# Decode attention over two caches: moving score products from the matrix engine's path to the vector path, with row sums on ScalarE

## The chip, the cores and the metric

One core of a Trainium2 chip runs the whole program. The metric is the device time of one execution in microseconds (us). Engines are named as in the profile: PE (matmul), PEld (its weight loads), DVE (VectorE), ACT (ScalarE), POOL (GpSimd) and SP (here only the issuer of the loads). "DMA engine" always means one of the 16 that move the data.

## The reference

Two independent attentions, A and B, each decode one token: 32 heads, 8192 cached keys of 128 numbers, bf16. The outputs of both are laid side by side.

```python
q = (x @ wq).reshape(B, 1, 32, 128).transpose(0, 2, 1, 3)   # x: 1 x 1 x 512
scores = einsum("bhqd,bhkd->bhqk", q, k_cache) * 128 ** -0.5 # k_cache: 1 x 32 x 8192 x 128
p = softmax(scores)
o = einsum("bhqk,bhkd->bhqd", p, v_cache)
out = o.transpose(0, 2, 1, 3).reshape(B, 1, 4096) @ wo       # wo: 4096 x 512
# result: concatenate([out_A, out_B], -1), 1 x 1 x 1024
```

Every cached byte is used once: K and V are 2 MB per head each, for 64 heads; with wq and wo that is 285 MB.

## The kernel before

The 64 heads are numbered through. Scores are made in rounds of 8 heads; one softmax serves a round. SP issues all loads in one order: in step g the V of head g - 12, then the K of head g, and once in a round one wo block of 1 MB. Four K slots and four V slots lie in SBUF.

Scores of a head go one of two ways. On **path P**, PE transposes K (64 tiles of 128x128), ACT copies the result out of PSUM, PE multiplies with q. On **path D** K stays as it is: it is multiplied by q, replicated over the partitions, and each group of 128 products is summed. POOL multiplies four of eight chunks, DVE the other four, and DVE sums all eight.

```python
def _default_path(NG, G, LAG):
    pre = "PDPDPPDPDPDP"                     # first 12 heads
    ...                                      # then every fourth head P: 20 P, 44 D in all

def load_v(g):
    if g >= NV:
        W('SP', c_pv, pv_val[g - NV])        # slot is free when PV of head g-4 is done
    ...
def load_k(g):
    if g >= NK:
        for ctr, val in k_free[g - NK]:      # slot is free when head g-4 has been multiplied / transposed
            W('SP', ctr, val)
    ...

def plan_D_step(g, u):                       # u = 0..7, one chunk each
    ...
    # DVE: chunks 4..7 multiplied, one per u     -> ybufe, "dmul"
    # POOL: chunks 0..3 multiplied, one per u    -> ybuf,  "mul"
    # DVE: chunk u summed with tensor_reduce     -> s_sb,  "red"

def plan_sm_tr(r, m1v):                      # softmax of round r, on PE
    W('PE', c_m1, m1v)                       # waits for DVE's maxima of all 8 heads
    ...
    OP('PE', lambda e: e.transpose(misc[:, 0:P], m1pad[:], ident_f[:])...)

def plan_PV(g, first, count):                # p times V of a head: 2 of 16 matmuls per u, on PE
    ...                                      # the last one frees V slot g % 4
```

In the timelines of this case PE runs its instructions in program order (at the tail, below, it stands idle for 6.73 us before the transpose although later PV matmuls need nothing from it).

## Time and profile before

| | before |
|---|---|
| time given, median of 4 runs | 687.79 us (687.55 to 688.66) |
| span of the profiled run, mean granted PE clock | 686.9 us, 0.807 |
| bytes loaded | 285.2 MB |
| share of the span in which the main load queue was busy | 99.0% |

The first fence has lines of the page: busy time, share of the span and instruction count of each engine; then two rows of 40 equal slices of the span (mean busy share of the DMA engines in tenths, and GB/s); then the DMA queues with packets, MB and share.

```profile
PE 447.7 (65%) x4107; PEld 265.4 (39%) x4163; DVE 525.4 (76%) x640; ACT 269.8 (39%) x534; POOL 372.1 (54%) x190
DMA  8999999999999999999999999999999999999995
GB/s 333 424 412 411 427 425 405 432 426 427 426 426 417 427 429 424 428 413 426 426 428 429 413 426 427 428 418 423 427 425 428 408 427 428 427 429 394 426 429 238
q1 hardware_dynamic: 28868, 285.23, 99.0%
q8 instruction: 33, 0.54, 0.3%
q14 instruction: 14, 0.11, 0.0%
```

No compute engine is close to full, and the loads are: the DMA share is 9 tenths or more in 38 of 40 slices. The Trainium skill ("Perfetto Trace Analysis", section Roofline) gives a core's 16 DMA engines about 435 GB/s together; the best slice here has 432, so the trace agrees. Two lines, q8 and q14, carry the instructions of the engines themselves. They are 0.65 MB of 286.

The second view is the groups of instructions (line, engine, operation, output and input with shapes, count; then busy us and mean ns of one; then idle time before them and what ended it).

```profile
L503 POOL TENSOR_TENSOR ybuf<-kn,qbc 128x1024 bf16<-128x1024 bf16 x176 | 367.8, 2121 | 246.2 <-DMA kn<-in_B_k_cache_dram 127.4
L512 DVE TENSOR_REDUCE s_sb<-ybuf 128x8 f32<-128x1024 bf16 x176 | 212.4, 1207 | 19.1 <-POOL ybuf L503 19.1
L524 DVE TENSOR_REDUCE s_sb<-ybufe 128x8 f32<-128x1024 bf16 x176 | 202.0, 1201 | 0.0
```

DVE's sums are the costliest thing it does: 414 of its 525 us. They would be the bottleneck if more heads went on path D. POOL mostly waits for K.

### The profile page before, as it was taken

What the parts mean: (1) busy time and instruction counts of PE and PEld (TensorE: products, weight loads), DVE (VectorE), ACT (ScalarE), POOL (GpSimd) and SP (SyncE); (2) the same over time, 40 slices, a digit from 0 to 9 for tenths busy, and PEclk for the clock granted to TensorE, in tenths of its full rate; (3) what the DMA queues carried; (4) which work ended last, traced back from release to release, by engine and by line L of the source; (5) the groups of instructions that cost most, each with busy time, mean ns of one, the idle gap of its engine ahead of it and who ended that gap; (6) DMA issues with size and microseconds to landing.
All of it is one profiled execution on the core that took longest, in us unless ns stands there. A gap on an engine that the chain in (4) does not pass through costs nothing.

```text
span 686.9 us, 10246 instructions
## 1 busy us (share of the span) xinstructions
PE 447.7 (65%) x4107; PEld 265.4 (39%) x4163; DVE 525.4 (76%) x640; ACT 269.8 (39%) x534; POOL 372.1 (54%) x190
## 2 busy tenths in 40 slices
PE   1577557845776658676566656675577654848985
PEld 1466555422524224252333325243253422415433
DVE  0356779999897897969989696996979789796001
ACT  0548657422625233262431426133262423415410
POOL 2434667567482755836486473845838376590000
PEclk9967857988698878788787887678778787887999
DMA  8999999999999999999999999999999999999995
GB/s 333 424 412 411 427 425 405 432 426 427 426 426 417 427 429 424 428 413 426 426 428 429 413 426 427 428 418 423 427 425 428 408 427 428 427 429 394 426 429 238
DMA packets 28915, 285.88 MB, mean 416 GB/s; under 512 B 3266, under 2 KB 11460, under 8 KB 11460
## 3 DMA queue, kind: packets, MB, share of 16 engines
q1 hardware_dynamic: 28868, 285.23, 99.0%
q8 instruction: 33, 0.54, 0.3%
q14 instruction: 14, 0.11, 0.0%
HBM read 285.21 MB, written 0.00 MB: 415 GB/s over the span
## 4 chain that ended last, share of the span: by engine, by line
DMA 49%; DVE 19%; PE 16%; issue 7%; ACT 5%; POOL 2%; SPq 1%; another core or an unknown queue 0%; ACTq 0%; DVEq 0%
DMA kn<-in_B_k_cache_dram 32%; DMA kn<-in_A_k_cache_dram 11%; DVE s_sb L512 9%; PE acc L716 8%; DVE s_sb L524 5%; DMA vn<-in_B_v_cache_dram 4%; PE ktps L409 4%; DVE ybufe L485 4%; ACT ktsb L418 3%; POOL ybuf L503 2%; PE misc L848 2%; DMA vn<-in_A_wq_dram 2%; DVE m1pad L599 1%; PE sps L442 1%; ACT ptmp L658 1%
## 5 line engine op out<-in xcount | busy, mean ns | idle before, releaser
L503 POOL TENSOR_TENSOR ybuf<-kn,qbc 128x1024 bf16<-128x1024 bf16 x176 | 367.8, 2121 | 246.2 <-DMA kn<-in_B_k_cache_dram 127.4
L716 PE MATMUL acc<-vn,pt 128*128 128x512 bf16 x939 | 274.7, 430 | 9.9 <-DMA vn<-in_B_v_cache_dram 5.1
L512 DVE TENSOR_REDUCE s_sb<-ybuf 128x8 f32<-128x1024 bf16 x176 | 212.4, 1207 | 19.1 <-POOL ybuf L503 19.1
L524 DVE TENSOR_REDUCE s_sb<-ybufe 128x8 f32<-128x1024 bf16 x176 | 202.0, 1201 | 0.0
L418 ACT COPY ktsb<-ktps 128x1024 bf16<-128x1024 bf16 x160 | 158.5, 1015 | 86.0 <-PE ktps L409 81.1
L409 PE MATMUL ktps<-ident,kn 128*128 128x128 bf16 x1280 | 126.9, 260 | 98.4 <-DMA kn<-in_B_k_cache_dram 60.3
L485 DVE TENSOR_TENSOR ybufe<-kn,qps 128x1024 bf16<-128x1024 bf16 x176 | 117.9, 670 | 63.1 <-issue 36.4
L409 PEld LDWEIGHTS ktps<-ident,kn 128*128 128x128 bf16 x1280 | 104.9, 119 | 141.1 <-DMA kn<-in_B_k_cache_dram 64.2
L716 PEld LDWEIGHTS acc<-vn,pt 128*128 128x128 bf16 x992 | 97.7, 109 | 107.2 <-issue 37.2
L796 ACT CAST accsb<-acc 4x512 bf16<-4x512 f32 x62 | 35.7, 576 | 218.6 <-PE acc L716 218.2
L442 PE MATMUL sps<-q_sb,ktsb 128*128 128x8 bf16 (+1 forms) x1280 | 57.1, 169 | 2.5 <-ACT ktsb L418 1.9
L442 PEld LDWEIGHTS sps<-q_sb,ktsb 128*128 128x128 bf16 x1280 | 52.3, 100 | 9.4 <-ACT ktsb L418 6.0
L689 ACT ACTIVATE pt<-ptmp,rinv 128x64 bf16<-128x64 f32 x64 | 16.1, 334 | 65.6 <-DVE rinv L676 65.6
L831 DVE CAST ot_pad<-misc 128x4 bf16<-128x4 f32 (+1 forms) x16 | 2.7, 168 | 39.9 <-PE misc L814 39.9
L848 PE MATMUL misc<-wo_sb,ot_pad 128*128 128x512 bf16 x62 | 22.3, 526 | 12.7 <-DVE ot_pad L831 12.7
L609 PE MATMUL misc<-ident_f,m1pad 128*128 128x128 f32 x8 | 3.5, 438 | 32.6 <-DVE m1pad L599 32.6
L374 PE MATMUL misc<-diag,ones_bf 128*128 128x512 bf16 (+3 forms) x14 | 5.1, 361 | 24.0 <-ACT diag L366 24.0
L334 PE MATMUL acc<-xT,vn 128*128 128x1 bf16 x256 | 7.1, 165 | 19.4 <-DMA vn<-in_A_wq_dram 14.9
L366 ACT ACTIVATE diag<-ident,q 128x128 bf16<-128x128 bf16 x44 | 14.5, 393 | 12.5 <-DVE q L348 12.5
L562 PE MATMUL qps<-ident,qrep 128*128 128x128 bf16 x44 | 4.0, 227 | 21.7 <-ACT qrep L545 21.7
L848 PEld LDWEIGHTS misc<-wo_sb,ot_pad 128*128 128x128 bf16 x64 | 7.5, 125 | 26.5 <-DVE ot_pad L831 15.2
L609 PEld LDWEIGHTS misc<-ident_f,m1pad 128*128 128x128 f32 x8 | 1.4, 172 | 36.3 <-DVE m1pad L599 36.3
(44 smaller groups left out, 123.2 us busy)
## 6 DMA issues: line engine op xcount, KB each, us to landing
kn<-in_A_k_cache_dram SPq DMA_DIRECT2D x32, 2048.0 KB, 22.5
vn<-in_A_v_cache_dram SPq DMA_DIRECT2D x32, 2048.0 KB, 23.4
kn<-in_B_k_cache_dram SPq DMA_DIRECT2D x32, 2048.0 KB, 27.8
vn<-in_B_v_cache_dram SPq DMA_DIRECT2D x32, 2048.0 KB, 23.6
vn<-in_A_wq_dram SPq DMA_DIRECT2D x1, 4096.0 KB, 12.9
vn<-in_B_wq_dram SPq DMA_DIRECT2D x1, 4096.0 KB, 17.4
wo_sb<-in_A_wo_dram SPq DMA_DIRECT2D x4, 1024.0 KB, 25.8
wo_sb<-in_B_wo_dram SPq DMA_DIRECT2D x4, 1024.0 KB, 29.6
```

The lines of the kernel that those rows point to most:

```text
L366: ins = e.activation(diag[:, db, i, :], ident[:], AF.Copy, scale=q32[:, h_:h_ + 1])
L409: last = e.transpose(ktps[:, bank, i * P:(i + 1) * P], kn[:, slot, t, :], ident[:])
L418: OP('ACT', lambda e, bank=bank, ks_slot=ks_slot: e.copy(ktsb[:, ks_slot, :], ktps[:, bank, :]).then_inc(c_e.sem, 1), "evac(%d,%d)" % (g, u))
L442: last = e.matmul(sps[:, sb, col:col + nn], ktsb[:, ks_slot, i * P:(i + 1) * P], q_sb[:, g:g + 1].broadcast_to([P, nn]), start=True, stop= ...
L485: OP('DVE', lambda e, slot=slot, es=es, i=i, qs=qs: e.tensor_tensor(ybufe[:, es], kn[:, slot, i * CH:(i + 1) * CH, :], qps[:, None, qs * P ...
L503: OP('POOL', lambda e, slot=slot, ys=ys, i=i, buf=buf, qi=qi: e.tensor_tensor(ybuf[:, ys], kn[:, slot, i * CH:(i + 1) * CH, :], qbc[:, buf ...
L512: OP('DVE', lambda e, ys=ys, rb=rb, j=j, i=i: e.tensor_reduce(s_sb[:, rb, j, i * CH:(i + 1) * CH], ybuf[:, ys], AX.X, ALU.add).then_inc(c_ ...
L524: OP('DVE', lambda e, es=es, rb=rb, j=j, i=i: e.tensor_reduce(s_sb[:, rb, j, i * CH:(i + 1) * CH], ybufe[:, es], AX.X, ALU.add).then_inc(c ...
L689: OP('ACT', lambda e, r=r, j=j, rb=rb: e.activation(pt[:, rb, j * NT:(j + 1) * NT], ptmp[:, rb, j, :], AF.Copy, scale=rinv[:, r, j:j + 1], ...
L716: last = e.matmul(acc[:, ob, :], pt[:, rb, j * NT - 32 * (j % XG) + c * PVC:j * NT - 32 * (j % XG) + c * PVC + P], vn[:, slot, c * PVC:(c ...
L796: OP('ACT', lambda e, ob=ob, xb=xb, k=k: e.copy(accsb[32 * k:32 * k + PVC, xb, :], acc[32 * k:32 * k + PVC, ob, :]).then_inc(c_ac.sem, 1), ...
L848: last = e.matmul(misc[:, 0:NOUT], ot_pad[:, g - r * G, :], wo_sb[:, r % 2, g - r * G, :], start=(i == 0), stop=(i == n - 1),)
```

## The change

The intent: nearly all heads go on path D (58 instead of 44; only heads 0, 2, 4, 6, 8 and 10 stay on P), which takes transposes off PE and copies off ACT. To make room on DVE, ACT sums two of the eight chunks, tile by tile, with `accum_out` (16 tiles per head, two instructions each). The four DVE multiplies move to the head's start, and the sums of POOL's chunks are planned a step later. The loads are not touched. In the cut below `LAG` is 12, `u` is one eighth of a head's step.

```diff
 def _default_path(NG, G, LAG):
-    pre = "PDPDPPDPDPDP"
     out = []
     for g in range(NG):
-        if g < len(pre):
-            out.append(pre[g])
+        if g < LAG:
+            out.append("P" if g % 2 == 0 else "D")
         else:
-            out.append("P" if ((g - len(pre)) % 4 == 3) else "D")
+            out.append("D")
 ...
+    ARC: int = 2,          # chunks of a head that ACT sums
+    ARC_PRE: int = 0,      # the same for the first NPRE heads
+    NPRE: int = 12,
 ...                        # in plan_D_step:
-            if DSTEP <= u < DSTEP + DVC:
-                i = NPC + (u - DSTEP)      # one DVE multiply per u
+            if u == 0:
+                for e_ in range(DVC):      # all four at u == 0
+                    i = NPC + e_
 ...
-                W('DVE', c_mul, mv)        # sum right after POOL's multiply
+                pend_red.append((g, n, i)) # sum a step later
 ...
+            for e_ in range(ARCg):
+                if u == min(UPH - 1, 1 + 2 * e_):
+                    i = NPC + e_
+                    ...
+                    for tt in range(CH):   # 8 tiles of 128 columns
+                        OP('ACT', lambda e, ...: e.activation(
+                            junk_a[:, ja, :], ybufe[:, es, tt, :], AF.Copy,
+                            accum_out=s_sb[:, rb, j, t:t + 1],
+                        ).then_inc(c_ared.sem, 1), "ared(%d,%d)" % (g, t), 2)
+            for e_ in range(ARCg, DVC):    # the other chunks: DVE tensor_reduce as before
 ...
```

## The prediction

> **What bounds it now.** The DMA. The page's slice row gives a DMA share of 9 tenths or more in 38 of 40 slices, mostly about 427 GB/s, and the main queue is busy 99.0% of the span with 285.2 MB. The Trainium skill ("Perfetto Trace Analysis", Roofline) gives about 435 GB/s for a core's 16 DMA engines; the best slice here reaches 432, so there is no headroom. The chain of waits repeats every 81.7 us: a round of 8 heads, K and V and one wo, at 424 GB/s, 10.2 us per head. In such a round the windows view shows DVE busy 71 us, PE 53 (clock 0.8), POOL 50, ACT 30.5: none is full, except DVE in an early round (79.3 of 81.7).
>
> **The change.** Path P (PE transposes, ACT evacuations) falls from 20 heads to 6, path D (POOL and DVE multiply, then reduce) rises from 44 to 58; from head 12 on all are D, and there ACT sums two of eight chunks instead of DVE. The four DVE multiplies move to the head's start. No byte of DMA changes.
>
> **Costs, from the timeline's pitches.** A 128x1024 reduction issues every 1.13 us, a DVE multiply every 0.59, a POOL multiply takes 2.12 (2.110 to 2.137).
> - DVE, D head: before 8 x 1.13 + 4 x 0.59 = 11.4 us; after 6 x 1.13 + 4 x 0.59 = 9.1. Round: 73 + 2.5 of softmax and output + 1 to 3 of waits = 77 to 79.
> - POOL: 68 per round.
> - ACT: exp pairs (activate 64 columns, accumulator read) issue every 0.336 us. "ScalarE: Activation LUTs" (What ACT_TABLE_LOAD costs) says 0.833 ns per element; my estimate for 128 columns is 0.39. Sixteen tiles: 6.2 us per head, 65 per round with the rest. 8.1 us of evacuations per P head go.
> - PE: 2560 transposes and QK matmuls become 768, off the path.
>
> All stay below 81.7, so the middle stays DMA-bound. DVE will run 2 to 10 us behind K's landing; four K buffers (about 40 us) hide that.
>
> **Ends.** First 12 heads: D takes 11.4 to 14 us per two heads against 9.8 of K; DVE falls 8 to 10 us behind and recovers later. Head 8 (P) now gates K12: its transposes wait behind round 0's maximum, which waits for D7, so K12 is issued near 93 us with the queue almost dry: 0 to 2 us lost, in place of the dip before (DMA share 0.96 at 102 to 119 us). The last head becomes D: the last softmax ends 0 to 4 us later, but V60's load needs the PV of head 56 only by about 9 us later than it came before. The end still follows the last V's landing (682 us).
>
> **Prediction:** 688.0 us, 8 in 10 within 685.5 to 692. Faster by over 2%: 0.01; within 2%: 0.94; slower by over 2%: 0.05.
>
> **What would show it.** DMA share 9 in nearly all slices; rounds of 81 to 82 us; per round DVE busy about 76, ACT 65, POOL 68; ACT sum pairs at 0.3 to 0.4 us; SP still waiting mostly for PV.
>
> **What would make it wrong.** ACT tiles at 0.55 us or more (accumulator read not overlapped) would fill ACT with 90 us a round and bound the kernel; DVE waits of over 6 us a round (multiplies waiting for ACT to free buffers, softmax steps queued behind ACT sums) would make DVE the bound; POOL slowed by the DVE bursts; a larger DMA gap near 95 us.

## The result, and the profile after

| | before | after |
|---|---|---|
| median | 688.28 us of 13 (687.55 to 689.78) | 694.81 us of 8 (693.75 to 695.3) |
| ratio | | 1.0094 (95%: 1.0084 to 1.0104) |
| span of the profiled run, PE clock | 686.9 us, 0.807 | 693.2 us, 0.763 |

All ratios in this document are the mean time of one kernel's runs over that of the kernel before in the same rounds, so not quite the ratio of the medians beside them. Executions over 1.5% slower than the fastest of the same kernel are left out of the means. The change costs 6.5 us, clear of the noise (the interval of the ratio lies above 1), and the prediction's range (685.5 to 692) does not hold it.

The same lines of the page after:

```profile
PE 369.5 (53%) x2356; PEld 180.9 (26%) x2385; DVE 569.3 (82%) x704; ACT 413.5 (60%) x2114; POOL 489.1 (71%) x246
DMA  8999999999999999999999999999999899999995
GB/s 335 424 412 414 425 419 428 428 427 428 426 428 413 428 429 425 428 415 426 427 429 419 421 427 430 425 415 427 429 426 427 317 432 427 429 421 390 360 428 222
q1 hardware_dynamic: 28868, 285.23, 98.3%
q8 instruction: 19, 0.31, 0.2%
q14 instruction: 27, 0.22, 0.1%
```

The same load packets, the same MB, and still no full engine. But one slice near 545 us has 317 GB/s and one from 641 to 659 us has 360. And the two instruction queues have changed places: 14 packets fewer on q8, 13 more on q14.

The groups after:

```profile
L519 POOL TENSOR_TENSOR ybuf<-kn,qbc 128x1024 bf16<-128x1024 bf16 x232 | 484.8, 2122 | 143.2 <-DMA kn<-in_B_k_cache_dram 64.6
L551 ACT ACTIVATE junk_a<-ybufe 128x128 bf16<-128x128 bf16 x832 | 243.7, 294 | 116.3 <-DVE ybufe L501 116.3
L530 DVE TENSOR_REDUCE s_sb<-ybuf 128x8 f32<-128x1024 bf16 x232 | 271.8, 1207 | 29.3 <-POOL ybuf L519 29.2
L551 ACT ACTIVATION_READ_ACCUMULATOR junk_a<-ybufe 128x1 f32 x832 | 155.2, 186 | 0.0
L566 DVE TENSOR_REDUCE s_sb<-ybufe 128x8 f32<-128x1024 bf16 x128 | 148.4, 1202 | 0.0
```

The compute came out as intended: DVE's sums take 420 us where they took 414, though 14 more heads use them; POOL's multiply is unchanged at 2122 ns; with its sums ACT is busy for 60% of the span.

**When did the bytes arrive?** The trace has a record of every DMA packet, so one can ask at which time X MB had landed:

```
MB landed            40     45    100    225    230    260    265    270    275   285.2
before, us        99.69 112.40 241.90 536.77 549.06 619.43 632.04 644.26 655.94 681.22
after - before    +0.28  -0.77  -0.84  -1.17  +2.71  +2.44  +3.37  +5.15  +5.62  +5.93
```

After the change the kernel is *ahead* for 540 us. It then loses 3.9 us within 5 MB (545 to 552 us), and about 3 us more between 630 and 650. Everything else is neutral. So two short places need explaining, not the middle.

**The first place: SP's queue.** The timeline of SP, before: start, duration, the issue. Its last line is the next load after the wait.

```profile
520.30 0.43 SPq L258 DMA_DIRECT2D wo_sb<-in_B_wo_dram  x1
528.38 16.44 SPq L258 DMA_DIRECT2D vn<-in_B_v_cache_dram  x1
544.92 0.38 SPq L258 DMA_DIRECT2D kn<-in_B_k_cache_dram  x1
```

And after:

```profile
524.74 0.43 SPq L263 DMA_DIRECT2D wo_sb<-in_B_wo_dram  x1
533.51 15.27 SPq L263 DMA_DIRECT2D vn<-in_B_v_cache_dram  x1
548.88 0.38 SPq L263 DMA_DIRECT2D kn<-in_B_k_cache_dram  x1
```

In both kernels an issue that follows a wo load hangs, for 10 to 17 us from the third wo load on, where most issues take 0.33 to 0.43 us. Here it is the seventh wo load. A wo load is 1024 pieces of 1 KB (64 for each DMA engine; the 8192 in the expectation of e1 are those of all eight wo loads), a K or V load 128 pieces of 16 KB (8 for each). The hang is about the same; what differs is what is left in the queue when it ends. Counted from the packet records: before, about 1.2 MB and 45 of the small pieces per engine; after, 0.13 MB and 4.0 per engine on average, that is 64 in all, exactly the share of *one* engine. The windows view says the same (window in us; its length; busy us and instruction count of PE, PEld, DVE, ACT, POOL; PE clock; DMA share; GB/s). Before:

```profile
546.00:548.00 2.00, 1.93 (x36) 1.60 (x36) 0.00 (x0) 1.87 (x3) 0.00 (x0) 1.00 0.96 364
548.00:550.00 2.00, 1.32 (x20) 0.74 (x17) 0.00 (x0) 1.91 (x3) 1.98 (x1) 1.00 1.13 431
```

After:

```profile
544.00:546.00 2.00, 0.00 (x0) 0.00 (x0) 2.00 (x4) 1.57 (x11) 2.00 (x2) 0.94 0.79 286
546.00:548.00 2.00, 0.00 (x0) 0.00 (x0) 2.00 (x3) 2.00 (x15) 2.00 (x2) 0.50 0.32 116
548.00:550.00 2.00, 0.00 (x0) 0.00 (x0) 1.66 (x2) 1.95 (x11) 2.00 (x2) 0.50 0.57 130
```

The number of DMA engines with a packet in flight, us by us from 540 to 552 after, is 16.0 16.3 16.5 16.7 14.7 11.5 8.3 2.5 1.7 6.2 14.9 16.2; before it stays above 14.7. The engines do not finish together: most have run dry while one still has its share to do.

**The second place: the last softmax.** The timeline of PE at the tail, before (in brackets the idle time before and what ended it):

```profile
633.68 0.38 PE L716 MATMUL acc<-vn,pt 128*128 128x512 bf16 x1
634.02 0.33 PE L609 MATMUL misc<-ident_f,m1pad 128*128 128x128 f32 x1
634.18 2.75 PE L716 MATMUL acc<-vn,pt 128*128 128x512 bf16 x11
```

And after:

```profile
637.60 0.47 PE L652 MATMUL misc<-ident_f,m1pad 128*128 128x128 f32 x1 [6.73 <-DVE m1pad L642]
638.54 0.25 PE L857 MATMUL misc<-ejr,accsb 128*128 128x8 bf16 x4 [0.47 <-DVE mcol L661]
638.65 3.20 PE L759 MATMUL acc<-vn,pt 128*128 128x512 bf16 x8
```

The transpose of the last round's maxima stands in PE's program ahead of most of the PV matmuls of head 52. After, the last head is a D head, its maxima come at 637.5 us instead of 633.9, and PE waits 6.73 us. PV of head 52 frees the slot for V of head 56. SP's issue of that load, before and after:

```profile
636.11 0.33 SPq L258 DMA_DIRECT2D vn<-in_B_v_cache_dram  x1
643.31 0.33 SPq L263 DMA_DIRECT2D vn<-in_B_v_cache_dram  x1
```

So it comes 7.2 us later. (The expectation of e3 has 631.5 us for the kernel before; that is V of head 55.) From 642 to 645 us, 13.4, then 2.1, then 9.0 DMA engines are busy.

### The profile page after: what moved, and what is told of

Same layout as the page of the kernel before. It is cut to its first block, busy times and chain, and to the rows that moved or that the text cites. A ratio compares the mean times of both kernels' runs of the same rounds, so it can differ in the third digit from the quotient of the medians.

```text
span 693.2 us, 8450 instructions
## 1 busy us (share of the span) xinstructions
PE 369.5 (53%) x2356; PEld 180.9 (26%) x2385; DVE 569.3 (82%) x704; ACT 413.5 (60%) x2114; POOL 489.1 (71%) x246
## 4 chain that ended last, share of the span: by engine, by line
DMA 48%; DVE 22%; POOL 12%; PE 5%; another core or an unknown queue 4%; issue 4%; SPq 3%; ACT 2%; POOLq 0%
DMA kn<-in_B_k_cache_dram 26%; DMA kn<-in_A_k_cache_dram 16%; POOL ybuf L519 12%; DVE s_sb L530 8%; DVE s_sb L566 7%; DVE ybufe L501 6%; DMA vn<-in_B_v_cache_dram 4%; SPq L263 3%; PE acc L759 2%; DMA vn<-in_A_wq_dram 2%; ACT junk_a L551 1%; PE misc L891 1%; PE acc L339 1%; DVE m1pad L642 0%
## 5 line engine op out<-in xcount | busy, mean ns | idle before, releaser
L519 POOL TENSOR_TENSOR ybuf<-kn,qbc 128x1024 bf16<-128x1024 bf16 x232 | 484.8, 2122 | 143.2 <-DMA kn<-in_B_k_cache_dram 64.6
L551 ACT ACTIVATE junk_a<-ybufe 128x128 bf16<-128x128 bf16 x832 | 243.7, 294 | 116.3 <-DVE ybufe L501 116.3
L530 DVE TENSOR_REDUCE s_sb<-ybuf 128x8 f32<-128x1024 bf16 x232 | 271.8, 1207 | 29.3 <-POOL ybuf L519 29.2
L551 ACT ACTIVATION_READ_ACCUMULATOR junk_a<-ybufe 128x1 f32 x832 | 155.2, 186 | 0.0
L501 DVE TENSOR_TENSOR ybufe<-kn,qps 128x1024 bf16<-128x1024 bf16 x232 | 143.0, 674 | 13.1 <-DMA kn<-in_A_k_cache_dram 12.2
L566 DVE TENSOR_REDUCE s_sb<-ybufe 128x8 f32<-128x1024 bf16 x128 | 148.4, 1202 | 0.0
L423 ACT COPY ktsb<-ktps 128x1024 bf16<-128x1024 bf16 x48 | 46.0, 1022 | 28.8 <-PE ktps L414 28.5
L414 PE MATMUL ktps<-ident,kn 128*128 128x128 bf16 x384 | 40.1, 273 | 8.3 <-ACT ktsb L423 4.0
L414 PEld LDWEIGHTS ktps<-ident,kn 128*128 128x128 bf16 x384 | 31.8, 125 | 12.0 <-ACT ktsb L423 8.4
L701 ACT ACTIVATE ptmp<-s_sb,negb 128x64 f32<-128x64 f32 x58 | 19.4, 336 | 0.2
```

The lines of the kernel that those rows point to most:

```text
L414: last = e.transpose(ktps[:, bank, i * P:(i + 1) * P], kn[:, slot, t, :], ident[:])
L423: OP('ACT', lambda e, bank=bank, ks_slot=ks_slot: e.copy(ktsb[:, ks_slot, :], ktps[:, bank, :]).then_inc(c_e.sem, 1), "evac(%d,%d)" % (g, u))
L501: OP('DVE', lambda e, slot=slot, es=es, i=i, qs=qs: e.tensor_tensor(ybufe[:, es], kn[:, slot, i * CH:(i + 1) * CH, :], qps[:, None, qs * P ...
L519: OP('POOL', lambda e, slot=slot, ys=ys, i=i, buf=buf, qi=qi: e.tensor_tensor(ybuf[:, ys], kn[:, slot, i * CH:(i + 1) * CH, :], qbc[:, buf ...
L530: OP('DVE', lambda e, ys=n2 % NY, rb=r2 % 2, j=j2, i=i2: e.tensor_reduce(s_sb[:, rb, j, i * CH:(i + 1) * CH], ybuf[:, ys], AX.X, ALU.add). ...
L551: OP('ACT', lambda e, es=es, tt=tt, rb=rb, j=j, t=t, ja=na % NJA: e.activation(junk_a[:, ja, :], ybufe[:, es, tt, :], AF.Copy, accum_out=s ...
```

## Theories

1. *The queue at the wo load*: the issue of 15 us is itself the cost, and the change shifts it to a worse moment.
2. *The tail*: the late last softmax is the cost.
3. *Order*: bunching the DVE multiplies, or the new path pattern, delays K's slots.
4. *Instruction packets*: the added instructions are fetched by the same 16 DMA engines, each packet from one of them. A load is split evenly over the engines and its semaphore waits for all of them, so the engine that lost most time sets the pace. The loss shows where the queue has no slack.

Some of the expectations below name theories by letters; C is the tail there, and E the instruction packets. Fetches are the same instruction packets.

**Theory 4, seen in the trace.** A packet of 16 KB takes 614 ns at the median, so the 16 engines can be followed one by one by their marks of completion: each load leaves 16 in the trace, one per engine. In the trace of after, from 112 to 300 us, these engines were set back (the labels are only names within this window; marks of under 0.2 us, which come while a wo load passes, are left out):

```
packet fetched at, size    engine set back, by (us), seen at (us)
124.2   8 KB               5    0.69          129.2
136.0   8 KB               3    0.69          138.6
148.1   8 KB               5    0.73          149.5
156.2  16 KB              12    1.56          160.2
173.9   8 KB               6    0.97          178.6
175.7   8 KB              15    0.69          179.5
203.8  16 KB              10    1.55          209.1
211.9   8 KB              15    0.69          214.4
241.3   8 KB              15    0.68          242.5
255.1   8 KB               1    0.72          258.9
264.5  16 KB              13    1.08 + 0.46   265.6, 270.9
273.1   8 KB              14    0.97          280.4
275.8   8 KB              15    0.69          277.5
```

Each packet has its engine: a 16 KB packet sets one back by 1.55 us, an 8 KB packet by 0.68 to 0.73 us (twice by 0.97, for a reason I did not find), and the others neither wait nor gain. Nobody takes over the work of the late one. The 16 KB packets fall on changing engines. The 8 KB packets fall on several engines and so may come from more than one stream, but from 175.7 us on one engine, number 15 here, is hit every 33 us. The marks of the later loads show this engine set back 14 times from 179.5 to 600 us, each time by about 0.69 us.

Whose stream is that? After the change ACT runs 308 counted instructions in a round of 8 heads (window 431 to 512.7 us), and a round takes 81.7 us. The Trainium skill ("Perfetto Trace Analysis", section The 4-stage abstract model) says that instructions have 64 bytes. That makes 8 KB (128 instructions) in 34 us, as an estimate, close to the 33 seen. For the 16 KB packets, PE and PEld instructions per packet are 8270 / 33 = 251 before and 4741 / 19 = 250 after: 65 bytes each. These follow PE. So the change moves fetching from a stream that is spread over several engines to one that, as far as it was followed, meets the same engine each time.

## The experiments

Fourteen kernels ran, in four batches, each with its own runs of the kernel before (medians 688.47, 687.84, 687.98 and 688.12 us). "Fill" instructions work on constants and touch nothing that the result needs.

### Is it the queue? e1 and e2

Each wo load from the third on is issued in four quarters of 256 KB over four steps, in after (e1) and in before (e2), by the same edit:

```diff
-            wo_land[j] = dma(wo_sb[:, j % 2], src, s_wo[j % 2], label="wo%d" % j)
+            def piece(k):
+                v = dma(wo_sb[:, j % 2, k * hp:(k + 1) * hp], src[:, k * hp:(k + 1) * hp, :], ...)
+                ...
+            piece(0)
+            for k in range(1, pieces):
+                wo_pieces.append([k, piece])     # one more in each of the next steps
```

> The changed kernel with each later wo load (1 MB, 8192 runs of 1 KB) cut into four loads of two heads each, issued one per head step. Theory A (queue block): at each wo load SP's next issue hangs 10 to 16 us [...]; at the seventh wo the other engines ran dry meanwhile (DMA share 0.82 at 544 to 561 us), worth 3.9 us, and the last wo 0.9 us. Then here no issue longer than about 4 us after 110 us, no dip near 545 us, and 689.5 to 691 us (ratio to before 1.002 to 1.005). Rival B (lag: V is released late because PE waits for DVE, so the backlog is simply too thin): the cut changes nothing there, the dip stays and the time is 694 to 695.5 us.

> The kernel before with the same cut of the wo loads. Theory A: the issues of 10 to 16 us go as well, but before the change the queue never ran dry behind them, so at most 1 to 2 us are gained: 686.5 to 688.5 us (ratio 0.997 to 1.001). If wo's small packets themselves, and not the block, were the cost, both e1 and e2 would stay where their parents are.

Measured: e1 694.59 us, ratio 1.0093 (1.0078 to 1.0109); e2 688.31 us, 0.9996 (0.9983 to 1.0008). The expectation of e1 missed, that of e2 held. The loss at 545 us was gone, and at 260 MB the kernel was 1.35 us ahead of before; then it lost 7.6 us between 265 and 270 MB. The windows of e1 there (columns as above):

```profile
638.00:640.00 2.00, 1.54 (x9) 0.70 (x9) 0.45 (x2) 0.30 (x1) 0.00 (x0) 0.50 0.19 75
640.00:642.00 2.00, 2.00 (x7) 0.84 (x5) 0.00 (x0) 0.00 (x0) 0.00 (x0) 0.50 0.09 33
642.00:644.00 2.00, 2.00 (x12) 1.06 (x11) 0.00 (x0) 1.55 (x10) 0.00 (x0) 0.93 0.12 41
```

Shares of 0.09 and 0.12 are one or two engines of 16. Theory 1 falls: the wo load is a place where the lag of the late engine (its debt, for short) is paid, and if it is removed the debt is paid later, in full.

### Is it the tail? e3

```diff
-            out.append("D")
+            out.append("P" if g == NG - 1 else "D")
```

> The changed kernel with head 63 alone back on path P. Theory C (tail: PE executes in order, and the transpose of the last round's maxima stands in its stream ahead of most of PV 52; it waits for DVE to finish head 63 at 636.5 us, PE idles 6.7 us, V56 is issued at 643.3 instead of 631.5 us and the DMA runs dry at 642 to 646 us): the dip at 642 us goes or halves, 692 to 693.5 us (ratio 1.006 to 1.008). Rival D (the tail loss is only the consequence of the dip at 545 us, everything late by the same amount): 694.5 to 695.5 us.

Measured: 694.29 us, 1.0086 (1.0072 to 1.01). Missed: only half a microsecond came back. The loss at 545 us stayed (+2.7 us at 230 MB). The tail alone does not explain the result. Nor is e3 rid of a late tail: V of head 56 is issued at 640.59 us, 4.5 us later than before, and 1.6 us are still lost between 260 and 270 MB.

### Instructions alone, in the kernel before: e4 to e7

e4 leaves the kernel before as it is and adds 819 small sums on ACT (16 columns, of a constant), 1638 instructions:

```diff
+            if g >= 12 and u in (1, 3):
+                for tt in range(11 if u == 1 else 10):
+                    ...
+                    OP('ACT', lambda e, ja=na % NJA: e.activation(
+                        junk_a[:, ja, :], ident[:, 0:16], AF.Copy,
+                        accum_out=junk_s[:, ja:ja + 1],
+                    ).then_inc(c_ared.sem, 1), "dummy(%d,%d)" % (g, na), 2)
```

e5 has 429 such sums (11 and 0), e6 1248 (16 and 16). e7 has the 429 of e5 on ACT and 819 small memsets on POOL, so that the packets of q14 are as many as in e4 but come from another engine:

```diff
+            if g >= 12 and u in (0, 2):
+                for tt in range(11 if u == 0 else 10):
+                    ...
+                    OP('POOL', lambda e, jp=npf % NJA: e.memset(
+                        junk_p[:, jp, :], 0.0).then_inc(c_pfill.sem, 1), ...)
```

> The kernel before with 819 extra small ACT sums (16 columns each with accumulator read, on data that never changes, waiting for nobody) placed as in the changed kernel, so ACT's instruction stream grows as it does there while DVE, POOL and PE work stay as before. Theory E (the instruction stream of ACT is fetched by DMA in 8 KB packets that hold up single DMA engines; the more fetches, the further the slowest engine falls behind, and the queue block at wo then empties the others): a dip at the sixth or seventh wo, instruction packets of the third queue kind from 14 to about 25, 689.5 to 692.5 us. Rival F (the skew comes from elsewhere or it is DVE's lag): no dip, 687.5 to 688.8 us.

> The kernel before with 429 instead of 819 extra ACT sums. Theory E, sharpened (the DMA packets show that each 8 KB fetch of instructions sets back one single DMA engine by about 0.7 us, each 16 KB fetch one engine by 1.55 us; the 16 KB ones go round eight engines, those of ACT fall about always on the same one; the loads are split evenly over 16 engines, so the kernel ends with the most delayed one): before, the worst engine bears about 6 us of 16 KB fetches and ACT's about 3.5; 6 more fetches for ACT make 7.6, so only 1 to 2.5 us are lost: 689.3 to 690.8 us. If instead every added fetch cost the same, half of e4's loss: 691.4 us. If ACT's time and not its fetches mattered: 688 to 688.6.

> The kernel before with 1248 extra ACT sums (one and a half of e4). Theory E: 6 more fetches on the same engine than e4, 0.69 us each, so 4 us more than e4: 697.5 to 700 us, third-kind packets 32 or so. If e4's loss came from another thing that the extra sums trip once (an order of waits), about the same as e4: 694 to 696.

> The kernel before with as many extra instructions as e4, but half of them on ACT (429 sums, 858 instructions) and half on POOL (819 small memsets). Theory E with one DMA engine per instruction stream: the worst engine bears what it bears in e5, so 689.3 to 691 us. If the sum of all fetched bytes counts, or all streams share an engine, the same as e4: 694 to 695.5.

Measured:

| kernel | ACT / POOL instructions | q14 packets | median us | ratio (95%) |
|---|---|---|---|---|
| before | 534 / 190 | 14 | 688.47, 687.84 | |
| e5 | 1392 / 190 | 20 | 690.37 | 1.0032 (1.0019 to 1.0046) |
| e4 | 2172 / 190 | 26 | 694.57 | 1.0089 (1.0075 to 1.0103) |
| e6 | 3030 / 190 | 33 | 699.12 | 1.0159 (1.0144 to 1.0173) |
| e7 | 1392 / 1009 | 26 | 690.3 | 1.0034 (1.0022 to 1.0047) |

Lines of e4's page:

```profile
PE 447.6 (65%) x4107; PEld 266.7 (38%) x4163; DVE 525.3 (76%) x640; ACT 432.7 (62%) x2172; POOL 371.8 (54%) x190
q8 instruction: 33, 0.54, 0.3%
q14 instruction: 26, 0.21, 0.1%
```

And of e7's:

```profile
PE 457.0 (66%) x4163; PEld 266.0 (39%) x4163; DVE 525.2 (76%) x640; ACT 356.3 (52%) x1392; POOL 410.3 (60%) x1009
q8 instruction: 33, 0.54, 0.3%
q14 instruction: 26, 0.21, 0.1%
```

e4 does no more of the score work than before and loses as much as the change (its expectation named less, 689.5 to 692.5; those of e5, e6 and e7 held). It loses it at the same place, 3.1 us between 225 and 230 MB, while its PE clock is 0.817, so the lower clock of after (0.763) is not the cause. From e5 to e6 the loss grows by (1.0159 - 1.0032) x 687.8 = 8.7 us for 13 packets, 0.67 us per packet; a packet sets its engine back by 0.69 in the trace. e7 has as many q14 packets as e4 and loses no more than e5: packets for POOL do not add to ACT's debt. The marks below ("What came of it") show that they do not set back ACT's engine either.

The numbers also give the bytes: 1638 ACT instructions brought 12 packets of 8192 bytes, 60 bytes each.

### The change without its instructions: e8, and mixes of path and sums: e9 to e12

All are the kernel after with other parameters. e8: `ARC` 0 and every fourth head from 15 on on P, so that only the order of the operations and the first 12 heads differ from before. e9: `ARC` 1 and the last head of each round on P. e10: `ARC` 0 and nothing else. e11: `ARC` 0 and every fifth head on P. e12: e11 with head 63 on P too.

```diff
-            out.append("D")
+            out.append("P" if ((g - LAG) % 4 == 3) else "D")                      # e8
+            out.append("P" if (g % 8 == 7) else "D")                              # e9
+            out.append("P" if ((g - LAG) % 5 == 4) else "D")                      # e11
+            out.append("P" if ((g - LAG) % 5 == 4 or g == NG - 1) else "D")       # e12
-    ARC: int = 2,
+    ARC: int = 0,   # e8, e10, e11, e12;  1 in e9
```

> The changed kernel without any ACT sums (ARC 0), with its new order of the DVE work and its first 12 heads (P and D in turn), and from head 12 on every fourth head P as before the change: the part of the change without its instructions. Theory E: the gain of 0.8 to 1.2 us of the first 12 heads stays and the loss goes: 686.3 to 688 us. If the new order or DVE's lag cost time, 689 or more.

> The changed kernel with one instead of two ACT chunks per head (ARC 1) and head 7 of every round on path P, so that DVE still fits (7 x 10.3 us + 2.5 = 75 us per round of 81.7). ACT's instructions fall from 2114 to about 1250, third-kind packets from 27 to about 20. Theory E: 6 to 7 fetches fewer on ACT's engine, 0.69 us each, so most of the loss goes: 688 to 690.5 us. If all-D or the new order cost the time and not ACT's instructions: 692 or more.

> The changed kernel with ARC 0: all heads from 12 on are D and DVE reduces all eight chunks. DVE then needs 8 x 11.4 + 2.5 to 4 = 94 to 95 us per round of 81.7 us: DVE-bound from head 12 on, 6.5 rounds of 13 us more: 760 to 780 us. It shows what the ACT sums were for.

> As e8, but every fifth head from 12 on is P instead of every fourth: 16 P heads instead of 19, some 750 PE instructions fewer, about three 16 KB fetches of 1.55 us less spread over eight engines. Theory E: the worst engine bears 0.5 to 1.5 us less than in e8: 686.3 to 687.5 us; DVE, with 4 x 11.4 us in 51 us, still fits. If DVE's waits matter: 688 or more.

> e11 with head 63 on path P as well. e11 missed its forecast by 4.5 us: up to 260 MB it runs 0.2 to 1 us ahead of the kernel before, then loses 5.7 us at 640 to 646 us, where V56 is not yet requested. Theory C (tail: PE works in order, and PV of head 52, which frees the buffer for V56, stands behind the transpose of the last round's maxima, which waits for DVE to finish head 63 at 637.5 us, against 632.9 us in the kernel before): with head 63 on P, DVE is done with its last head earlier, the dip goes and 686.5 to 688.5 us come out. If the tail dip has another cause: 691 to 692.5 us.

| kernel | ACT instructions | q8 / q14 packets | median us | ratio (95%) |
|---|---|---|---|---|
| e8 | 528 | 32 / 14 | 687.79 | 0.9995 (0.9981 to 1.0008) |
| e9 | 1212 | 26 / 20 | 692.05 | 1.0059 (1.0046 to 1.0071) |
| e10 | 450 | 19 / 14 | 780.86 | 1.1347 (1.1326 to 1.1368) |
| e11 | 510 | 29 / 15 | 692.04 | 1.0054 (1.0041 to 1.0068) |
| e12 | 516 | 30 / 14 | 687.59 | 0.9996 (0.9983 to 1.0009) |

e8, as expected, settles theory 3: the new order costs nothing. e10 shows what ACT's sums buy: without them DVE sets the time, with 682 us busy (0.86 us over the expected range).

e9 and e11 missed their expectations, and taught the second half. Both are level with before or ahead of it until 265 MB (1.0 us and 0.3 us ahead) and lose everything at the tail. In e9 PE waits there 3.41 us for ACT's copies of head 63, which stand behind ACT's sums. In e11, with fewer ACT instructions than before (510 against 534), the last round's maxima come at 638 us, and the windows show the same famine:

```profile
638.00:640.00 2.00, 1.92 (x5) 0.81 (x6) 0.28 (x1) 0.30 (x1) 0.00 (x0) 0.50 0.50 213
640.00:642.00 2.00, 2.00 (x6) 0.76 (x5) 0.00 (x0) 0.00 (x0) 0.00 (x0) 0.50 0.10 41
642.00:644.00 2.00, 2.00 (x7) 1.03 (x6) 0.00 (x0) 0.31 (x1) 0.00 (x0) 0.52 0.02 8
```

e12 changes one head of e11, the last: the maxima come at 630.3 us, and the same three windows of e12 have shares of 1.00, 1.01 and 1.05. So the late last softmax costs 4.0 us (by the ratios) to 4.4 us (by the medians, 692.04 - 687.59) by itself. In e12, as expected, the loss is gone. Together with e3 this makes a square:

| | last head on P | last head on D |
|---|---|---|
| few ACT instructions (every fifth head P, no ACT sums) | e12: 687.59 | e11: 692.04 |
| 2088 to 2114 ACT instructions (all D, ACT sums) | e3: 694.29 | after: 694.81 |

Either fault alone costs 4 to 7 us; both together cost only 0.5 us more than the larger. That they overlap is measured, with the reserve that e3 still has part of the late tail. While the other engines stand idle at the tail the late one catches up, so the idle time is paid once. The marks show it: from the load of V 55 to that of V 56 the last mark's distance from the median of the 16 falls from 4.72 to 2.51 us in after, and only from 3.97 to 3.50 us in e3.

### Once more with the kernel after: e13 and e14

The fills on top of after: 416 small sums on ACT (832 instructions, e13), or 832 memsets on POOL (e14).

```diff
+            if g >= 12 and u == 2:                  # e14: u in (0, 2)
+                for tt in range(8):
+                    ...
+                    OP('ACT', lambda e, jp=nf % NJA: e.activation(      # e14: 'POOL', e.memset(junk_f[:, jp, :], 0.0)
+                        junk_f[:, jp, :], ident[:, 0:16], AF.Copy,
+                        accum_out=junk_s[:, jp:jp + 1]).then_inc(c_fill.sem, 1), ..., 2)
```

> The changed kernel with 416 small ACT sums more (832 instructions, some 6.5 fetches of 8 KB). Theory E: the changed kernel is bound by the DMA engine that carries ACT's instructions, so each adds 0.69 us: 698 to 700.5 us. If the changed kernel's loss is due to something else (lag of DVE, tail), under 696.5 us.

> The changed kernel with 832 small POOL memsets more: as many added instructions as in e13, on the other stream. Theory E: they load another DMA engine, which bears less than ACT's, so next to nothing is lost: 694 to 696 us. If the sum of fetched instructions counts: as e13.

Measured: e13 699.5 us, 1.0164 (1.015 to 1.0178), 33 q14 packets; e14 694.85 us, 1.01 (1.0084 to 1.0115), 34. Both expectations held. Six more packets for ACT cost 4.7 us over after, 0.78 each; seven more for POOL cost nothing. In e13's trace one engine is set back by about 0.69 us at seven places between 139 and 280 us, one every 22.5 us where after has 33. At the wo load it is then left alone:

```profile
546.00:548.00 2.00, 0.00 (x0) 0.00 (x0) 2.00 (x4) 0.04 (x1) 2.00 (x1) 0.88 0.78 259
548.00:550.00 2.00, 0.00 (x0) 0.00 (x0) 2.00 (x4) 2.00 (x14) 2.00 (x2) 0.50 0.12 46
550.00:552.00 2.00, 0.00 (x0) 0.00 (x0) 1.97 (x2) 2.00 (x21) 2.00 (x2) 0.50 0.06 25
```

A share of 0.06 is exactly one engine of 16: for two microseconds the whole kernel waits for it.

### What came of it

The debt can be read from the kept traces. For each run, the last of a load's 16 marks minus their median, taken at the last load that had landed by 530 us, before the small pieces of the seventh wo load pass:

| | before | e8 | e5 | e7 | e4 | after | e14 | e6 | e13 |
|---|---|---|---|---|---|---|---|---|---|
| ACT instructions | 534 | 528 | 1392 | 1392 | 2172 | 2114 | 2114 | 3030 | 2946 |
| POOL instructions | 190 | 194 | 190 | 1009 | 190 | 246 | 1078 | 190 | 246 |
| lag of the last engine, us | 2.2 | 1.8 | 3.2 | 3.1 | 6.8 | 7.3 | 6.9 | 8.9 | 10.1 |

With few ACT instructions the lag scatters (0.9 us in e12, 3.5 in e11); above that it follows ACT's instructions and not POOL's (e7 against e5, e14 against after), and the times of these nine follow it. From before to after it grows by 5.1 us, where the kernel loses 6.5; more packets meet the late engine after this point, and the tail adds its part. No version was clearly faster than before; e8 and e12 equal it.

## Why the prediction was wrong

- **Right: what bounds the kernel.** The DMA bounds it before and after, and the middle rounds stayed at the DMA's pace: after is ahead by about 1 us until 536 us.
- **Right: the engine costs.** POOL's multiply was predicted at 2.12 us and took 2122 ns. DVE's sums fell from 9.4 to 7.2 us per D head (414.4 / 44 and 420.2 / 58), and DVE did not bound the middle rounds: in a round of 81.7 us it was busy for 75.6 us on average (predicted 76), POOL for 65.7 (68), ACT for 53.6 (65). One ACT tile was estimated at 0.39 us and was faster: the sums start every 0.292 us. The Trainium skill ("ScalarE: Activation LUTs", section What ACT_TABLE_LOAD costs) says that each 128x1 pointer operand adds about 93 ns. My estimate came from exp pairs of 64 columns (one every 0.331 us; the prediction read 0.336), which have such a bias; the sums have none. 0.331 + 64 x 0.000833 - 0.093 = 0.291, so the trace agrees with the page; I had used only half of what it says.
- **Right: the start.** K of head 12 was issued at 92.1 us (predicted near 93). It cost 0.3 us at 40 MB, and the old dip at 102 to 119 us, which went away, gave back 1 us.
- **Wrong: "No byte of DMA changes."** True of the loads, not of what the DMA engines carry. ACT's instructions went from 534 to 2114, q14 from 14 to 27 packets. In sum the instruction bytes even fell (0.65 to 0.53 MB); what counts is that the added ones meet the same engine each time, that its lag adds up over the whole run, and that every load waits for the last engine. e4, e5, e6 and e13 show it with nothing else changed. This is the step that failed first.
- **Wrong: "V60's load needs the PV of head 56 only by about 9 us later than it came before."** This followed the data and forgot the program order of PE. The transpose of the last maxima stands ahead of most of PV of head 52, and so gates V of head 56, which came 7.2 us later. e11 against e12 puts the cost at 4.0 to 4.4 us where ACT's stream is short. In the kernel after it hides behind the first fault (e3).
- **The listed risks** (slow ACT tiles, DVE waits, POOL slowed by DVE, a gap at 95 us) did not come. The one that did was not on the list. The "off the path" verdict for PE's transposes and QK matmuls was right in its effect (at the tail PE's order did matter): 14 fewer packets of 16 KB brought no visible gain, since e8, which has 32 of them, is ahead of before by 0.7 us at 225 MB as well, against 1.2 after.

## What to carry to other kernels

Where loads fill all DMA engines, count instructions as traffic: compare the instruction queues' packets and the instruction counts of each engine before and after, because many tiny instructions on one engine can delay one DMA engine and with it every load. When the loads run short, look at the DMA share in windows of 2 us: 0.06 of 16 engines is one engine that all others wait for, and the place where this shows (here a wo load of many small pieces, or the tail) need not be where it was caused. And for each slot that a load waits for, read what stands ahead of its release in the program order of the engine that frees it, not only its data.

## What the Trainium skill lacked or had wrong

- "DMA: Bandwidth & Descriptors" (section Queues, rings and completion order) lists a runtime-internal queue row whose uses include refill, and says that an engine alternates between its rows. This section gives no cost, and no page has a measured one. Here each 8 KB instruction packet set back one DMA engine by 0.69 us and each 16 KB packet by 1.55 us, and the others not at all.
- No page says that one engine's instruction stream can meet the same DMA engine every time (the point belongs to "Runtime: NRT & Kernel Launch", section Instruction fetch mechanics). In the two traces followed, ACT's did (every 33 us in after, every 22.5 in e13), at 0.67 to 0.78 us of kernel time per packet, while PE's 16 KB packets changed engines.
- "DMA: Bandwidth & Descriptors" does not say that an issue can hang behind a load of many small pieces: after the seventh wo load, of 1024 pieces of 1 KB, the next issue took 16.44 us before and 15.27 us after the change, instead of 0.33.
- "ScalarE: Activation LUTs" (What ACT_TABLE_LOAD costs) has the 93 ns of a pointer operand and agrees with the runs. It does not give the pitch of an activation with its accumulator read: 0.292 us for 128 columns without a pointer operand, 0.331 us for 64 columns with one.
